# Cumulative decays in SBUF buffers of their own, and three chunks masked away from VectorE

## The chip, the cores and the metric

The kernel runs on one core of a Trainium2 chip. The metric is the device time of one execution in microseconds (us). Before the change the median of three runs is 357.06 us (356.91 to 357.37). The profile shown is one execution of 357.22 us; its instructions span 355.1 us.

## The reference

Two layers stand behind one another. The first is a gated linear attention over 4 batches, 8 heads, 768 steps and head size 48. The second is a channel mix with widths 384 and 1024.

```python
f = 1.0 / (1.0 + np.exp(-f_logit))
for t in range(S):
    state = f[:, :, t, :, None] * state + np.einsum('bhd,bhe->bhde', k[:, :, t], v[:, :, t])
    y[:, :, t] = np.einsum('bhd,bhde->bhe', q[:, :, t], state)
# x is y with its heads side by side; x_prev is x one step earlier (0 for the first)
xk = mu_k * x + (1.0 - mu_k) * x_prev
xr = mu_r * x + (1.0 - mu_r) * x_prev
k = np.maximum(xk @ w_k, 0.0)
out = sigmoid(xr @ w_r) * (k * k @ w_v)
```

All of it is float32; mu_r and w_r are drawn 8 times as large as the other inputs of their kind, so the kernel keeps each matrix operand as a high and a low part and multiplies three of the four combinations.

## The kernel before

**Chunks.** The 768 steps of a batch are cut into 6 chunks of 128, so there are 24 chunks, numbered i. A chunk's tiles have 128 partitions (two heads) by 4 pairs by 128 steps, that is 512 float32 for each partition. For a chunk the tasks are, with the names that the code gives them: `b` (L240) is a scan on VectorE that multiplies the gates up to cumulative decays; `bl` (L243, L244) copies its last column; `ln` and `rb` (L246, L248) on ScalarE make the reciprocal of the decays; `q` (L250) multiplies q by b; `kr` (L258, L259) multiplies k by the reciprocal, on GpSimd as a rule; `n` and `k` (L270, then three instructions at L262 and L266) correct that reciprocal with one Newton step, where `n` writes its product over b. Then TensorE transposes k (`TR`, L310), a copy takes it out of PSUM (`kt`, L314 or L315), and `SP` (L325, L345) makes the scores of the chunk with itself and the state's increment in `pss`. `m` (L337) masks the scores on VectorE and writes them to `ss`. For chunks below AWAY, ScalarE copies the scores out (L332), and `mg` on GpSimd masks them in SBUF (L334). `za`, `zb`, `T` (L290, L296, L302) carry the state, `YA` and `YB` (L362) make y in `py`, and `y` (L394 on ScalarE, L396 on VectorE) takes it out.

**Units.** Three chunks are a unit u of 384 steps; there are 8. Six small transfers per unit (`sp`, L452) spread y into x. The mix is `d` (L464), `xm` (L482; L477 and L474 for unit 0), the high part `xh` (L491 or L490), the low part `xl` (L497, GpSimd). TensorE makes 8 blocks `F` of nine 128x384 matrix products each, 3 blocks `R` of nine, and 6 half blocks `W` of twelve (all at L505). Between F and W the result is rectified, squared and split (`r` L528 or L529, `h` L533, `kk` L535 or L537, `l` L543 on GpSimd). `o` (L595) is the last product.

**Weights.** They arrive as 64 bit words. Eighteen pieces (8 of wk, 4 of wr, 6 of wv) are turned into float32 by three VectorE instructions, S, T and X (L623, L632, L635), then split by ScalarE (`H`, L638) and GpSimd (`L`, L642). `F`, `R` and `W` of the first unit wait for their pieces.

**PSUM.** Of eight banks, `pss` and `py` hold two each. The other four are the shared pool `pm`, from which a task takes a bank: b of a chunk from its scan to the last instruction of `k`; the transposed k; d; each word piece from S to X; each F, R and W block.

**Order.** Every engine's order is fixed when the program is made. `Plan.schedule` simulates the five queues (P TensorE, V VectorE, A ScalarE, G GpSimd, Q the SyncE queue of the DMAs). It takes, time after time, the task that can start first, in steps of 0.15 us; ties go to the lower `place`. Places are given in units: `ga = i/3 - LEAD - GATE` for the front of a chunk, `at = i/3 - LEAD` for its back, `u - PREP` for the mix, and WORDS and PLACE for weights and single loads. A task with several ways (engine, time, port flag) takes the one with the lowest end plus `DEAR` of its engine. With the port flag set, a VectorE task is lengthened by half of what GpSimd still has to run, at most to double. HAND and DRAIN are the planner's allowances for a semaphore and for TensorE's results. From chunk TIED on, `YB` waits for the next chunk's `SP`, so that small products stand together. Idle TensorE time that the planner foresees early in the program is filled with products of the identity (L700).

Of the kernel before, what the change touches and what calls it, by code (L numbers as in the profile page):

```python
# [33 lines left out]
BUFS = {  # L34
    "pm": (4, [512]), "rb": (2, [NP, C]), "ss": (2, [2, NP, C // 2]), "ktk": (2, [NP, 2, D]), "v": (3, [H, D]),
    "x": (3, [KJ, 1 + UT]), "stage": (2, [1, UT]), "xm": (4, [UT]), "r": (2, [UT]), "kk": (2, [UT]),
# [6 lines left out]

LEAD, GATE, PREP = 1.669, 0.274, 0.51
WORDS = {"wk": (-0.282, 0.023), "wr": (-4.892, 0.005), "wv": (-0.241, 0.052)}
HAND, DRAIN = 0.136, 0.465
TURN = {(True, False): 0.125, (False, True): 0.2}
TIED = 8
FILL = (14.0, 0.85)
LATE = {"sp": 3.3, "qk": 1.9}  # L50
BUNDLE = True
AWAY = 1
SPLIT = True
HALVED = 1
PLACE = {"f1": -0.627, "f2": 0.21, "sf2": -1.016, "qk0": 0.854, "qk1": -0.278, "qk2": 0.127, "qk3": 0.31, "v0": -0.151, "v1": -0.224, "cst": 0.482, "mu": 0.138, "f3": -1.807}
CHECK = (2.0, 0.2)
DEAR = {"V": 2.498, "A": 2.512}


class Plan:  # L60
# [23 lines left out]
    def schedule(self, trace=None):  # L84
        free = {"P": 0.0, "V": 2.2, "A": 0.0, "G": 1.0, "Q": 0.7}
# [22 lines left out]
        while ready:  # L108
            best = None
            for n, names in ready.items():  # L110
                _, place, ways, _, takes, _ = self.tasks[n]
                at = 0.0
                if any(not slots[b[0]] for b in takes):
                    continue
                for b in takes:
                    at = max(at, min(slots[b[0]])[0])
                at = {w[0]: max([at] + [0.0 if way_of[m] == w[0] else end[m] for m in names]) for w in ways}
                pick = min(((max(at[w[0]], free[w[0]]) + w[1] + DEAR.get(w[0], 0.0), w) for w in ways), key=lambda x: x[0])[1]
                start = max(at[pick[0]], free[pick[0]])
# [72 lines left out]
class Rwkv:  # L192


    wk = wr = wv = None
# [7 lines left out]
    def b(self, *key):  # L203
        return self.tiles[key[0]][self.slot[key]]
# [10 lines left out]
    def add_attention(self, pl, i):  # L215
# [19 lines left out]
        f = lambda: self.f_t[u % NFB][:, c]  # L235
        b = lambda: self.b("pm", ("b", i)).rearrange("p (a c) -> p a c", a=NP)
        rb = lambda: self.b("rb", i)
# [3 lines left out]
            b().rearrange(FL), f().rearrange(FL), self.low.rearrange(FL), 1.0, op0=ALU.mult, op1=ALU.max)),  # L241
            after=[f"sf{u}.{c}" if u == 0 else f"sf{u}"], takes=[("pm", ("b", i))])
        pl.add(f"bl{i}", ga, ("A", 0.2, 0, lambda: nc.scalar.copy(self.bl[:, i], b()[:, :, C - 1])),  # L243
               ("V", 0.15, 0, lambda: nc.vector.tensor_copy(self.bl[:, i], b()[:, :, C - 1])),  # L244
               uses=[("pm", ("b", i))])
        pl.add(f"ln{i}", ga, ("A", 0.63, 0, lambda: nc.scalar.activation(rb(), b(), AF.Ln)),  # L246
               after=["ex"], takes=[("rb", i)], uses=[("pm", ("b", i))])
        pl.add(f"rb{i}", ga, ("A", 0.63, 0, lambda: nc.scalar.activation(rb(), rb(), AF.Exp, scale=-1.0)),  # L248
               after=I("ln"), uses=[("rb", i)])
        pl.add(f"q{i}", ga, ("V", 0.69, 0, lambda: nc.vector.tensor_tensor(q(), q(), b(), op=ALU.mult)),  # L250
               after=I("qk"), uses=[("pm", ("b", i))])

# [8 lines left out]
        def k_b():  # L261
            nc.vector.scalar_tensor_tensor(  # L262
                k()[:, ::2], b()[:, ::2], 2.0, k()[:, ::2], op0=ALU.subtract, op1=ALU.mult)
            for h in (0, 1):
# [680 lines left out]
```

## Time and profile before

| | |
|---|---|
| median of 3 runs | 357.06 us |
| profiled execution | 357.22 us, span 355.1 us |
| busy TensorE / VectorE / ScalarE / GpSimd | 320.0 / 260.3 / 201.5 / 196.5 us |
| of TensorE: filling products | 10.8 us |
| first transpose, first F product, last o | 19.94, 51.33, 349.25 us |

The profile of one execution has a page with busy times, a strip of the span in 40 slices, the chain that ended last and the costliest groups. The trace behind it gives single instructions (start, duration, engine, line, operands, and what ended the engine's idle time in brackets), sums for chosen stretches of time, and the least, middle and largest duration of the instructions of a line. A line number is the place of the instruction in the kernel above.

### The profile page before, as it was taken

The numbers are of one execution on the slowest core, as the hardware profiler recorded it, in microseconds if no ns is written. First come the engines' busy times: TensorE is split into PE (matmuls) and PEld (weight loads), VectorE is DVE, ScalarE is ACT, GpSimd is POOL, SyncE is SP. The second block draws the span as 40 slices with busy tenths as digits, with TensorE's granted clock in tenths as the row PEclk, the third lists the DMA queues.
The fourth block names the chain that finished last, engine by engine and source line by source line (L and its number), as shares of the span: only waits on it lengthen the run. The fifth ranks groups of instructions, "written<-read, shape, count | busy, mean of one in ns | idle before, by whom it ended". The sixth has DMA issues, their size and how long they took to land.

```text
span 355.1 us, 10862 instructions
## 1 busy us (share of the span) xinstructions
PE 320.0 (90%) x4482; PEld 304.0 (86%) x4482; DVE 260.3 (73%) x526; ACT 201.5 (57%) x400; POOL 196.5 (55%) x235
## 2 busy tenths in 40 slices
PE   0294678999999999999999999999999999999993
PEld 0283567888989999999999999999999999999992
DVE  7887699989998798877999788848973943723110
ACT  3786358758367827844467537772676156605520
POOL 2555459985779357733677267725790634634400
PEclk9999899999999999999999999999999999999998
DMA  7999462336451363366323632131401100010001
GB/s 260 398 378 372 162 223 65 106 105 209 118 185 59 127 226 129 123 236 221 117 81 116 212 128 89 46 121 52 160 1 38 50 27 11 9 46 22 3 24 52
DMA packets 20650, 45.32 MB, mean 128 GB/s; under 512 B 2928, under 2 KB 13040, under 8 KB 20592
## 3 DMA queue, kind: packets, MB, share of 16 engines
q1 hardware_dynamic: 20592, 44.55, 37.0%
q8 instruction: 37, 0.61, 0.7%
q14 instruction: 21, 0.17, 0.1%
HBM read 38.64 MB, written 4.72 MB: 122 GB/s over the span
## 4 chain that ended last, share of the span: by engine, by line
PE 68%; DVE 13%; ACT 5%; issue 4%; DMA 3%; POOL 3%; SPq 1%; DVEq 0%; POOLq 0%; ACTq 0%
PE pm L505 55%; PE py L362 6%; PE pm L310 3%; PE pss L325 2%; DMA f<-in_zt 2%; DVE pm L632 2%; PE pss L345 2%; DVE pm L623 2%; POOL k2l L543 1%; DVE xm L482 1%; DVE ss L337 1%; DMA words<-in_wv 1%; DVE xm L477 1%; DVE words L635 1%; DVE xh L491 1%
## 5 line engine op out<-in xcount | busy, mean ns | idle before, releaser
L505 PE MATMUL pm<-xh,wk 128*128 128x384 f32 x384 | 105.3, 344 | 1.5 <-POOL wk L642 1.1
L505 PE MATMUL pm<-wv,k2h 128*128 128x384 f32 x384 | 98.6, 338 | 0.0
L543 POOL TENSOR_TENSOR k2l<-kk,k2h 128x384 fp32r<-128x384 f32 x64 | 68.5, 1075 | 32.2 <-DVE kk L535 16.3
L497 POOL TENSOR_TENSOR xl<-xm,xh 128x384 fp32r<-128x384 f32 x48 | 52.5, 1095 | 60.4 <-DVE xh L491 54.6
L505 PEld LDWEIGHTS pm<-xh,wk 128*128 128x128 f32 x384 | 69.8, 188 | 4.4 <-POOL wk L642 2.0
L505 PEld LDWEIGHTS pm<-wv,k2h 128*128 128x128 f32 x384 | 68.7, 188 | 0.3
L505 PE MATMUL pm<-xl,wk 128*128 128x384 f32 x192 | 64.6, 337 | 0.0
L505 PE MATMUL pm<-wv,k2l 128*128 128x384 f32 x192 | 64.5, 336 | 0.0
L528 ACT ACTIVATE r<-pm 128x384 f32<-128x384 f32 x54 | 26.5, 490 | 34.0 <-PE pm L505 33.3
L505 PE MATMUL pm<-wr,xh 128*128 128x384 f32 x144 | 38.0, 345 | 1.0 <-DVE words L635 0.9
L505 PEld LDWEIGHTS pm<-wv,k2l 128*128 128x128 f32 x192 | 36.1, 188 | 0.0
L595 DVE TENSOR_TENSOR o<-pm,lg 128x384 f32<-128x384 f32 x24 | 13.3, 553 | 31.1 <-PE pm L505 30.9
L505 PEld LDWEIGHTS pm<-xl,wk 128*128 128x128 f32 x192 | 36.1, 188 | 0.0
L535 DVE SCALAR_TENSOR_TENSOR kk<-pm,r 128x384 f32<-128x384 f32 x38 | 21.1, 554 | 20.0 <-ACT r L528 18.8
L533 ACT ACTIVATE k2h<-r 128x384 fp32r<-128x384 f32 x64 | 33.6, 524 | 3.5 <-DVE r L529 1.2
L240 DVE TENSOR_TENSOR_SCAN pm<-f,low 128x512 f32<-128x512 f32 x24 | 32.7, 1363 | 0.1
L362 PE MATMUL py<-qk,z 64*64 64x64 f32 x704 | 22.9, 230 | 10.0 <-issue 3.3
L362 PEld LDWEIGHTS py<-qk,z 64*64 64x64 f32 x704 | 16.4, 135 | 18.0 <-issue 8.8
L505 PEld LDWEIGHTS pm<-wr,xh 128*128 128x128 f32 x144 | 25.2, 188 | 1.9 <-DVE words L635 1.0
L482 DVE SCALAR_TENSOR_TENSOR xm<-pm,mu_sb,x 128x384 f32<-128x384 f32 x42 | 25.7, 612 | 0.7
L700 PE MATMUL py<-ident 128*128 128x64 f32 x72 | 10.8, 310 | 15.4 <-DMA ident<-in_cst 15.4
L505 PE MATMUL pm<-wr,xl 128*128 128x384 f32 x72 | 24.2, 336 | 0.0
(101 smaller groups left out, 559.2 us busy)
## 6 DMA issues: line engine op xcount, KB each, us to landing
qk<-in_qkt SPq DMA_DIRECT2D x24, 512.0 KB, 4.3
words<-in_wv SPq DMA_DIRECT2D x12, 512.0 KB, 3.9
f<-in_zt SPq DMA_DIRECT2D x7, 768.0 KB, 5.2
v<-in_vt SPq DMA_DIRECT2D x24, 192.0 KB, 3.1
out<-o SPq DMA_DIRECT2D x24, 192.0 KB, 2.6
words<-in_wk SPq DMA_DIRECT2D x6, 512.0 KB, 5.4
words_k2h<-in_wk SPq DMA_DIRECT2D x4, 384.0 KB, 8.6
words_k2l<-in_wk SPq DMA_DIRECT2D x4, 384.0 KB, 9.4
```

Of the source, the lines that this page charges most:

```text
L240: pl.add(f"b{i}", ga, ("V", 1.25, 1, lambda: nc.vector.tensor_tensor_scan(b().rearrange(FL), f().rearrange(FL), self.low.rearrange(FL), 1. ...
L310: nc.tensor.transpose(pk()[:, j], k()[:, j], self.ident)
L362: first[c, h] = nc.tensor.matmul(to, lhs, rhs, start=(c, h) not in first, stop=stop, skip_group_check=True)
L482: pl.add(f"xm{u}.{n}{j}", pr, ("V", 0.62, 0, lambda xm=xm, n=n, j=j: nc.vector.scalar_tensor_tensor(xm(), pm("d", u, j)[:, :UT], self.mu_s ...
L497: e.tensor_tensor(lo(), xm(), hi().bitcast(F32), op=ALU.subtract)
L505: nc.tensor.matmul(ps, lhs(a, j), rhs(bb, j), start=ends[0] and i == 0, stop=ends[1] and i == len(pr) - 1)
L528: pl.add(f"r{u}.{f}", kf, ("A", 0.5, 0, lambda r=r, ps=ps: nc.scalar.activation(r(), ps(), AF.Relu)), ("V", 0.56, 0, lambda r=r, ps=ps: nc ...
L533: pl.add(f"h{u}.{f}", kf, ("A", 0.53, 0, lambda r=r, hi=hi: nc.scalar.activation(hi(), r(), AF.Square)), after=[f"r{u}.{f}"], **kw)
L535: pl.add(f"kk{u}.{f}", kf, ("V", 0.56, 0, lambda r=r, ps=ps, kk=kk: nc.vector.scalar_tensor_tensor(kk(), ps(), 0.0, r(), op0=ALU.max, op1= ...
L543: e.tensor_tensor(lo(), kk(), hi().bitcast(F32), op=ALU.subtract)
L595: pl.add(f"o{u}.{t}", kv, ("V", 0.56, 0, lambda t=t, ps=ps, o=o: nc.vector.tensor_tensor(o(), ps(), lg()[:, t], op=ALU.mult)), after=[f"W{ ...
L700: self.nc.tensor.matmul(self.py[:, 0, 256:320], self.ident, self.ident[:, :64], start=False, stop=True, skip_group_check=True)
```

## The change

The tile b gets a pool of its own of three SBUF buffers, `"b": (3, [512])`, and no longer takes a bank of `pm`. The scan, `q`, `n` and the three instructions of `k` have the same shapes and now work on SBUF operands alone. `q` and `n` get GpSimd as a second way, with a surcharge of its own in DEAR; `q`, `n` and `k` get the port flag. AWAY rises from 1 to 3: chunks 1 and 2 are masked by ScalarE and GpSimd as chunk 0 was. The planner's numbers change with it: PREP, HAND, DRAIN, TIED, DEAR, the place of the wr pieces and the places of nine loads or gates of the start. The order of all queues is planned anew from them.

```diff
 BUFS = {
-    "pm": (4, [512]), "rb": (2, [NP, C]), "ss": (2, [2, NP, C // 2]), ...
+    "pm": (4, [512]), "b": (3, [512]), "rb": (2, [NP, C]), "ss": (2, [2, NP, C // 2]), ...
-LEAD, GATE, PREP = 1.669, 0.274, 0.51
-WORDS = {"wk": (-0.282, 0.023), "wr": (-4.892, 0.005), "wv": (-0.241, 0.052)}
-HAND, DRAIN = 0.136, 0.465
+LEAD, GATE, PREP = 1.669, 0.274, 1.542
+WORDS = {"wk": (-0.282, 0.023), "wr": (-5.255, 0.025), "wv": (-0.241, 0.052)}
+HAND, DRAIN = 0.157, 0.419
-TIED = 8
+TIED = 7
-AWAY = 1
+AWAY = 3
-PLACE = {"f1": -0.627, "f2": 0.21, "sf2": -1.016, "qk0": 0.854, "qk1": -0.278, "qk2": 0.127, "qk3": 0.31, "v0": -0.151, "v1": -0.224, "cst": 0.482, "mu": 0.138, "f3": -1.807}
+PLACE = {"f1": -0.627, "f2": -0.161, "sf2": -1.73, "qk0": 0.284, "qk1": 0.836, "qk2": -0.619, "qk3": 0.263, "v0": -0.151, "v1": -0.236, "cst": 0.345, "mu": 0.138, "f3": -2.05}
-DEAR = {"V": 2.498, "A": 2.512}
+DEAR = {"V": 3.432, "A": 2.426, "qG": 4.083, "nG": 4.943}
...
-pick = min(((max(at[w[0]], free[w[0]]) + w[1] + DEAR.get(w[0], 0.0), w) for w in ways), key=lambda x: x[0])[1]
+pick = min(((max(at[w[0]], free[w[0]]) + w[1] + DEAR.get(w[0], 0.0) + DEAR.get(n[0] + w[0], 0.0), w) for w in ways), key=lambda x: x[0])[1]
...
-        b = lambda: self.b("pm", ("b", i)).rearrange("p (a c) -> p a c", a=NP)
+        b = lambda: self.b("b", i).rearrange("p (a c) -> p a c", a=NP)
...
-            after=[f"sf{u}.{c}" if u == 0 else f"sf{u}"], takes=[("pm", ("b", i))])
+            after=[f"sf{u}.{c}" if u == 0 else f"sf{u}"], takes=[("b", i)])
...
-        pl.add(f"q{i}", ga, ("V", 0.69, 0, lambda: nc.vector.tensor_tensor(q(), q(), b(), op=ALU.mult)),
-               after=I("qk"), uses=[("pm", ("b", i))])
+        pl.add(f"q{i}", ga, ("V", 0.69, 1, lambda: nc.vector.tensor_tensor(q(), q(), b(), op=ALU.mult)),
+               ("G", 1.3, 0, lambda: nc.gpsimd.tensor_tensor(q(), q(), b(), op=ALU.mult)),
+               after=I("qk"), uses=[("b", i)])
...
-        pl.add(f"n{i}", ga, ("V", 0.69, 0, lambda: nc.vector.tensor_tensor(b(), rb(), b(), op=ALU.mult)),
-               after=I("rb") + I("q") + I("bl"), uses=[("pm", ("b", i)), ("rb", i)])
-        pl.add(f"k{i}", ga, ("V", 0.98, 0, k_b), after=I("n") + I("kr"), uses=[("pm", ("b", i))])
+        pl.add(f"n{i}", ga, ("V", 0.69, 1, lambda: nc.vector.tensor_tensor(b(), rb(), b(), op=ALU.mult)),
+               ("G", 1.3, 0, lambda: nc.gpsimd.tensor_tensor(b(), rb(), b(), op=ALU.mult)),
+               after=I("rb") + I("q") + I("bl"), uses=[("b", i), ("rb", i)])
+        pl.add(f"k{i}", ga, ("V", 0.98, 1, k_b), after=I("n") + I("kr"), uses=[("b", i)])
```

More of the change, by code (lines that the diff above doesn't have):

```diff
@@ L34 @@
 BUFS = {
-    "pm": (4, [512]), "rb": (2, [NP, C]), "ss": (2, [2, NP, C // 2]), "ktk": (2, [NP, 2, D]), "v": (3, [H, D]),
+    "pm": (4, [512]), "b": (3, [512]), "rb": (2, [NP, C]), "ss": (2, [2, NP, C // 2]), "ktk": (2, [NP, 2, D]), "v": (3, [H, D]),
     "x": (3, [KJ, 1 + UT]), "stage": (2, [1, UT]), "xm": (4, [UT]), "r": (2, [UT]), "kk": (2, [UT]),
@@ L241, in add_attention @@
             b().rearrange(FL), f().rearrange(FL), self.low.rearrange(FL), 1.0, op0=ALU.mult, op1=ALU.max)),
-            after=[f"sf{u}.{c}" if u == 0 else f"sf{u}"], takes=[("pm", ("b", i))])
+            after=[f"sf{u}.{c}" if u == 0 else f"sf{u}"], takes=[("b", i)])
         pl.add(f"bl{i}", ga, ("A", 0.2, 0, lambda: nc.scalar.copy(self.bl[:, i], b()[:, :, C - 1])),
                ("V", 0.15, 0, lambda: nc.vector.tensor_copy(self.bl[:, i], b()[:, :, C - 1])),
-               uses=[("pm", ("b", i))])
+               uses=[("b", i)])
         pl.add(f"ln{i}", ga, ("A", 0.63, 0, lambda: nc.scalar.activation(rb(), b(), AF.Ln)),
-               after=["ex"], takes=[("rb", i)], uses=[("pm", ("b", i))])
+               after=["ex"], takes=[("rb", i)], uses=[("b", i)])
         pl.add(f"rb{i}", ga, ("A", 0.63, 0, lambda: nc.scalar.activation(rb(), rb(), AF.Exp, scale=-1.0)),
                after=I("ln"), uses=[("rb", i)])
-        pl.add(f"q{i}", ga, ("V", 0.69, 0, lambda: nc.vector.tensor_tensor(q(), q(), b(), op=ALU.mult)),
-               after=I("qk"), uses=[("pm", ("b", i))])
+        pl.add(f"q{i}", ga, ("V", 0.69, 1, lambda: nc.vector.tensor_tensor(q(), q(), b(), op=ALU.mult)),
+               ("G", 1.3, 0, lambda: nc.gpsimd.tensor_tensor(q(), q(), b(), op=ALU.mult)),
+               after=I("qk"), uses=[("b", i)])
         def halves(t):
```

## The prediction

> **What bounds the kernel now.** I read the page's strip first, then sums of busy time by stretch, then the chain that ended last, then single instructions. The strip has 8.9 us in a digit.
>
> ```profile
> span 355.1 us, 10862 instructions
> ...
> PE   0294678999999999999999999999999999999993
> ```
>
> TensorE (PE) climbs for nine slices and then stays at 9. The stretches say the same in microseconds; behind the length stand the busy times of TensorE, of its weight loads, of VectorE, ScalarE and GpSimd, and at the end granted clock, DMA share and GB/s.
>
> ```profile
> 0.00:20.00 20.00, 3.71 (x17) 3.55 (x17) 16.24 (x33) 10.93 (x16) 9.04 (x18) 1.00 0.91 335
> 20.00:45.00 25.00, 16.89 (x571) 14.49 (x575) 19.32 (x45) 15.76 (x37) 11.46 (x20) 0.93 0.83 291
> 45.00:60.00 15.00, 12.25 (x204) 10.83 (x197) 14.59 (x30) 10.26 (x23) 10.88 (x12) 1.00 0.50 169
> 60.00:82.50 22.50, 20.83 (x180) 18.87 (x179) 20.84 (x37) 16.68 (x33) 20.93 (x20) 1.00 0.30 91
> 82.50:100.00 17.50, 17.32 (x268) 15.64 (x267) 16.24 (x35) 9.89 (x20) 10.40 (x14) 1.00 0.59 200
> 100.00:248.00 148.00, 147.88 (x2181) 142.81 (x2180) 123.07 (x247) 88.66 (x175) 87.79 (x103) 1.00 0.39 131
> ```
>
> From 100 us on TensorE lacks 0.12 us in 148: nothing saved on another engine there can shorten the kernel. Between 45 and 82.5 us it is idle for 37.50 - 12.25 - 20.83 = 4.42 us, and part of its busy time is the planner's filling (same columns, for the filling's line alone, TensorE first):
>
> ```profile
> 45.00:60.00 15.00, 2.90 (x24) 2.90 (x24) 1.00 0.50 169
> 60.00:82.50 22.50, 2.89 (x24) 2.96 (x24) 1.00 0.30 91
> ```
>
> So 4.42 + 5.79 = 10.2 us of that stage are no work on the result. What TensorE waits for is in the chain of waits, in order of time (start, us, what):
>
> ```profile
> 52.85 0.68 DVE words L635
> ...
> 67.61 0.56 DVE words_k2l L635
> ...
> 297.30 51.93 PE pm L505 x297
> 349.25 0.56 DVE o L595
> ```
>
> Here the chain lies on VectorE's conversion of the weights, with VectorE busy 14.59 of 15 and 20.84 of 22.5 us; near the end it is TensorE alone. **The bound is VectorE's load from 20 us to about 100 us, and TensorE after it.** A microsecond off VectorE in that stage is worth up to a microsecond, until 10.2 us are used up.
>
> **The change part by part.** *Two masks leave VectorE.* The groups of the three instructions (busy us, mean ns), and the instructions round chunk 1's mask:
>
> ```profile
> L337 DVE TENSOR_TENSOR ss<-pss,mask 128x512 f32<-128x512 f32 x23 | 15.7, 684 | 2.5 <-PE pss L345 2.2
> L334 POOL TENSOR_TENSOR ss<-ss,mask 128x512 f32<-128x512 f32 x1 | 1.3, 1272 | 4.2 <-ACT ss L332 4.2
> L332 ACT COPY ss<-pss 128x512 f32<-128x512 f32 x1 | 0.6, 585 | 0.2 <-PE pss L345 0.2
> ...
> 26.31 0.68 DVE L337 TENSOR_TENSOR ss<-pss,mask 128x512 f32<-128x512 f32 x1
> 30.50 0.63 PE L362 MATMUL py<-ss,v 64*48 64x64 f32 x32
> ```
>
> VectorE loses 2 x 0.684 = 1.37 us, ScalarE gains 1.17, GpSimd (11.46 of 25 us busy) 2.54. The masked scores of chunk 1 come 0.585 + 1.272 - 0.684 = 1.17 us later; they lie ready from 26.99 to 30.50 us, so 3.5 us cover that, and I cost it at nothing. Without the cover it would be 1.17 us for y of that chunk. What is queued behind the mask on GpSimd is `kr` of the next chunks, 1.27 us later at worst, inside the same cover.
>
> *Scan, q, n and k work in SBUF.* Three lines of before tell what this does (least, middle and largest ns), with the means of the groups:
>
> ```profile
> L464 DVE TENSOR_TENSOR pm<-x x21: 553/567/1204, 83.7 to 307.4; 128x384 f32<-128x384 f32 x21
> L240 DVE TENSOR_TENSOR_SCAN pm<-f,low x24: 1218/1226/2094, 9.3 to 258.2; 128x512 f32<-128x512 f32 x24
> L250 DVE TENSOR_TENSOR qk<-qk,pm x24: 669/677/689, 12.3 to 259.8; 128x512 f32<-128x512 f32 x24
> L692 DVE TENSOR_REDUCE least<-words x15: 536/676/687, 107.4 to 228.4; 128x1 f32<-128x512 f32 x12, 128x1 f32<-128x384 f32 x3
> ...
> L240 DVE TENSOR_TENSOR_SCAN pm<-f,low 128x512 f32<-128x512 f32 x24 | 32.7, 1363 | 0.1
> L464 DVE TENSOR_TENSOR pm<-x 128x384 f32<-128x384 f32 x21 | 14.7, 698 | 7.2 <-DMA x<-stage 6.7 <-ACT lg L562 0.3
> ```
>
> With one operand in PSUM, q never varies (669 to 689). With both inputs in SBUF, d goes up to 1204 and the scan to 2094. What they wait for:
>
> ```profile
> 113.37 1.98 POOL L543 TENSOR_TENSOR k2l<-kk,k2h 128x384 fp32r<-128x384 f32 x2
> 115.32 1.12 POOL L287 TENSOR_TENSOR g<-bl,f 128x4 f32<-128x4 f32 x1
> ...
> 114.62 1.82 DVE L240 TENSOR_TENSOR_SCAN pm<-f,low 128x512 f32<-128x512 f32 x1
> ...
> L287 POOL TENSOR_TENSOR g<-bl,f x20: 192/203/1212, 12.7 to 260.5; 128x4 f32<-128x4 f32 x20
> ```
>
> The scan issued at 114.62 ends at 116.44, 1.09 us after GpSimd's k2l has ended, and the gate of four elements that GpSimd began at 115.32 ends with the scan, where a gate takes 0.20 as a rule. The two take turns by whole instructions. The mean over the least is 1363 - 1218 = 145 ns for the scan and 698 - 553 = 145 for d. q, n and the three instructions of k join this kind. In 20 to 100 us these are, in this order for q, n and the two lines of k:
>
> ```profile
> 20.00:100.00 80.00, 4.08 (x6) 0.98 0.57 192
> 20.00:100.00 80.00, 4.81 (x7) 0.98 0.57 192
> 20.00:100.00 80.00, 3.16 (x8) 0.98 0.57 192
> 20.00:100.00 80.00, 3.82 (x16) 0.98 0.57 192
> ```
>
> 37 instructions, 37 x 0.145 = **+5.4 us** on VectorE. The low end is nothing, where GpSimd happens to rest; the high end is half of a 1.0 us GpSimd instruction at GpSimd's share there (53.67 of 80 us), 37 x 0.335 = 12.4. I take the measured mean, since the scans and d fell in the same traffic. The instructions' own length I leave as it is: reading 512 elements from SBUF alone took 676 ns (the reduction), from SBUF and PSUM 677 (q).
>
> [...]
>
> *Banks come free.* A chunk's decays no longer hold one of four banks. What this can buy is VectorE's idle time in the stage; its two large pieces are
>
> ```profile
> 36.47 0.16 DVE L382 COPY done<-py 128x2 f32<-128x2 f32 x1 [2.04 <-PE py L362]
> 44.20 0.56 DVE L315 COPY ktk<-pm 128x384 f32<-128x384 f32 x1 [1.94 <-PE pm L310]
> ```
>
> with word pieces still to be converted. Both waits are for TensorE, in an order that was fixed beforehand, so a free bank fills them only if the new order sets word work in front of them. Between 0 and -3.98 us I take the middle, **-2.0**.
>
> *More work goes to ScalarE.* DEAR was 2.498 against 2.512, a tie; now VectorE is dearer by 1.0 us, so `kt` and `xh`, which have both ways, turn to ScalarE unless it is that much later. Their VectorE time, kt in 20 to 45 us and xh in 45 to 60:
>
> ```profile
> 20.00:45.00 25.00, 1.67 (x3) 0.93 0.83 291
> 45.00:60.00 15.00, 2.94 (x5) 1.00 0.50 169
> ```
>
> Together 4.61 us; ScalarE is idle 9.2 and 4.7 us in those stretches, so it can take them. Between 0 and 4.6 I take all of kt and four of five xh: **-4.0**. GpSimd's new ways for q and n cost 1.3 + 4.083 and 1.3 + 4.943 against VectorE's 0.69 + 3.432, so they are chosen only where VectorE is 1.3 or 2.1 us behind; I count none, and both ends of that lie inside the 5.4 us above.
>
> *Places and loads.* PREP puts the mix ahead of the chunks. Unit 0's first F could start earlier, but its blocks then wait for the words of wk, which VectorE makes; under its load this is worth nothing, and shows only where VectorE falls idle. The same holds for unit 1, whose blocks stand behind W of unit 0 on TensorE. The first loads change turns on SyncE: qk1 goes back by 1.1 units; qk2, qk0, f2, f3 and the wr pieces come forward. The bytes are the same, and the queue moves 335 GB/s there (the stretch 0 to 20), so a 0.5 MB load changed about is 1.6 us early or late: 0, with 1.6 either way, mostly covered by VectorE's queue. HAND, DRAIN and TIED are only numbers of the planner.
>
> **Sum:** -1.37 + 5.4 - 2.0 - 4.0 = -2.0 us. The profiled execution took 357.22 us, which is 0.16 above the median; 357.22 - 2.0 - 0.16 = **355.1 us**.
>
> **Rivals.** *A, slower: the turns between VectorE and GpSimd become the bound.* In 45 to 82.5 us GpSimd is busy 10.88 + 20.93 = 31.8 of 37.5 us. The locked VectorE work there is 2 scans and 5 casts xh (whose least is below); one chunk's q, n and k adds, at 0.68 + 0.69 + 0.98, 2.35 us more.
>
> ```profile
> L491 DVE CAST xh<-xm x38: 351/379/1003, 46.6 to 312.2; 128x384 fp32r<-128x384 f32 x38
> ...
> 100.00:248.00 148.00, 8.23 (x12) 1.00 0.39 131
> ```
>
> 31.8 + 2 x 1.22 + 5 x 0.35 + 2.35 = 38.3 of 37.5 us: over the top by 0.8 at least. Later, 12 chunks (the row of n) bring 28 us into the 60 us that GpSimd leaves free in 148, which scan, d and xh already use. If the wait of an instruction doubles to 0.29 us, 5.4 more come on: 357.06 - 2.0 + 5.4 = **360.5 us**. The point is where the mean wait passes 0.145 + 2.0/37 = 0.20 us. For it: the planner counts half of GpSimd's rest once for k's three instructions, and no wait of GpSimd at all. Against it: part of the 37 falls in 20 to 45 us, where GpSimd is busy 11.46 of 25 us.
> [...]
>
> *B, no change: the banks were not what held it, and ScalarE's share is eaten by the turns.* Then -1.37 - 4.0 + 5.4 = 0.0: **357.1 us**. For it: the two idle pieces wait for TensorE, not for a bank.
>
> *C, much faster: the freed banks let the words be done ahead.* Most of the 10.2 us comes back, some 8: **349 us**. For it: eighteen pieces of three instructions each hold a bank; against it: they cost VectorE the same time whenever they run.
>
> [...]
>
> **How the numbers follow.** Forecast 0.45, A 0.28, B 0.14, C 0.07, D 0.06. A measurement of this kernel tells about 0.2% (0.7 us) from no change. Faster 0.45 + 0.07 + 0.06 = 0.58, same 0.14, slower 0.28. The forecast's own range is 352 to 356.3 us. The bounds of the terms reach from -1.4 - 4.0 - 4.6 = -10 (capped by the 10.2 us) to -1.4 + 12.4 = +11; 8 in 10 leaves out most of C and the far part of A: **350 to 360.5 us**.
>
> **What would show it.** Right: q, n and k spread upwards like d, by 0.1 to 0.2 us in the mean, with least values as before; VectorE's kt and xh fall in 20 to 60 us; filling plus idle of TensorE in 45 to 82.5 us falls from 10.2 to about 8; TensorE stays full after 100 us. [...]

## The result: 1.0% slower, and the profile after

The changed kernel takes 360.73 us (median of 4 runs, 359.84 to 362.36), the kernel before in the same comparison 357.22 us (4 runs, 356.91 to 358.05). The ratio is 1.010, with a 95% interval of 1.0059 to 1.0140. The forecast was 355.1 us in a range of 350 to 360.5: the sign was wrong, and the time lies at the place of rival A. The profiled execution took 359.84 us, its span is 358.0 us.

The page of the changed kernel, its busy times and its strip (a digit is 8.95 us):

```profile
span 358.0 us, 10771 instructions
...
PE 325.3 (91%) x4482; PEld 308.9 (86%) x4482; DVE 243.9 (68%) x408; ACT 246.3 (69%) x518; POOL 216.6 (61%) x237
...
PE   0397679899999999999999999999999999999993
```

VectorE is busy 16.4 us less than before (260.3), and the kernel is slower. ScalarE has 44.8 us more, GpSimd 20.1 us more. The stretches of the prediction, of the changed kernel (length; TensorE, weight loads, VectorE, ScalarE, GpSimd; granted clock, DMA share, GB/s):

```profile
20.00:45.00 25.00, 19.44 (x529) 16.88 (x528) 21.30 (x36) 15.29 (x39) 17.84 (x22) 0.90 0.74 247
45.00:60.00 15.00, 12.65 (x229) 11.90 (x228) 14.40 (x30) 11.97 (x30) 9.64 (x11) 0.82 0.61 210
60.00:82.50 22.50, 20.80 (x174) 18.34 (x173) 21.34 (x33) 18.61 (x43) 21.69 (x20) 1.00 0.30 94
100.00:248.00 148.00, 147.10 (x2161) 141.50 (x2164) 115.16 (x190) 113.99 (x240) 97.76 (x103) 1.00 0.42 135
```

Two things differ from what the prediction looked for. Between 20 and 82.5 us VectorE is as full as it was (57.04 us against 54.75 before), although masks, kt and xh have left it. And after 100 us TensorE is no longer full: it lacks 0.90 us in 148, where it lacked 0.12.

What filled VectorE is seen in the groups of the changed kernel (busy us, mean ns | idle before and who ended it) and, below, in the least, middle and largest ns of their lines:

```profile
L240 DVE TENSOR_TENSOR_SCAN b<-f,low 128x512 f32<-128x512 f32 x24 | 35.2, 1475 | 1.5 <-ACT f L573 1.5
L260 POOL TENSOR_TENSOR qk<-qk,rb 128x256 f32<-128x256 f32 x24 | 23.6, 985 | 0.0
L250 DVE TENSOR_TENSOR qk<-qk,b 128x512 f32<-128x512 f32 x24 | 23.5, 984 | 6.1 <-DMA qk<-in_qkt 5.9
L267 DVE SCALAR_TENSOR_TENSOR qk<-b,qk 128x128 f32<-128x128 f32 x48 | 23.2, 523 | 0.0
L259 POOL TENSOR_TENSOR qk<-qk,rb 128x256 f32<-128x256 f32 x24 | 22.5, 938 | 10.4 <-ACT rb L248 9.6 <-DMA qk<-in_qkt 0.6
L271 DVE TENSOR_TENSOR b<-rb,b 128x512 f32<-128x512 f32 x24 | 21.3, 887 | 4.8 <-ACT rb L248 4.1
L263 DVE SCALAR_TENSOR_TENSOR qk<-b,qk 128x256 f32<-128x256 f32 x24 | 18.3, 764 | 3.3 <-POOL qk L259 1.9
```

```profile
L250 DVE TENSOR_TENSOR qk<-qk,b x24: 665/987/1625, 13.8 to 260.3; 128x512 f32<-128x512 f32 x24
L271 DVE TENSOR_TENSOR b<-rb,b x24: 679/852/1386, 16.9 to 261.4; 128x512 f32<-128x512 f32 x24
L263 DVE SCALAR_TENSOR_TENSOR qk<-b,qk x24: 416/736/1386, 18.2 to 262.6; 128x256 f32<-128x256 f32 x24
L267 DVE SCALAR_TENSOR_TENSOR qk<-b,qk x48: 276/280/1107, 19.1 to 264.6; 128x128 f32<-128x128 f32 x48
```

The least values stand where they stood (q 669 before, 665 now), and nearly everything above them is new (the largest before were 689 for q, 697 for n, 425 and 291 for `k`): the mean of `q` is 0.32 us over its least, `n` 0.21, the first instruction of `k` 0.35, each of the other two 0.25. For a chunk that is 0.32 + 0.21 + 0.35 + 2 x 0.25 = 1.38 us, in 24 chunks 33 us of VectorE's instructions. GpSimd pays too: the halves of `kr` (L259, L260) were 0.735 and 0.748 us before and are 0.938 and 0.985.

A piece of the timeline of the changed kernel, VectorE, then GpSimd (start, us), shows who meets whom:

```profile
22.56 0.69 DVE L271 TENSOR_TENSOR b<-rb,b 128x512 f32<-128x512 f32 x1 [0.29 <-ACT rb L248]
...
24.35 0.95 DVE L263 SCALAR_TENSOR_TENSOR qk<-b,qk 128x256 f32<-128x256 f32 x1
25.22 1.54 DVE L267 SCALAR_TENSOR_TENSOR qk<-b,qk 128x128 f32<-128x128 f32 x2
```

```profile
22.61 1.23 POOL L259 TENSOR_TENSOR qk<-qk,rb 128x256 f32<-128x256 f32 x1 [3.72 <-ACT rb L248]
23.80 1.22 POOL L260 TENSOR_TENSOR qk<-qk,rb 128x256 f32<-128x256 f32 x1
24.98 0.90 POOL L259 TENSOR_TENSOR qk<-qk,rb 128x256 f32<-128x256 f32 x1
```

`n` and the first half of `kr` both wait for `rb` (the releaser in the brackets is the same, ACT rb L248), so they start 0.05 us apart: `n` goes through in its 0.69, `kr` takes 1.23 in place of 0.74. Then `k` meets the halves of the next `kr`, and its two short instructions take 1.54 us where 2 x 0.28 is their length.

Such meetings behind one event are the smaller part, though. Over the whole trace `n` and the first half of `kr` start within 0.1 us of each other in only 4 of 24 chunks, and in those `n` loses nothing (0.68 and 0.69 us). Taking every one of the five instructions that lies more than 0.05 us above its least (32.6 us in all), and the GpSimd instruction that ran when it began, 13.5 us belong to `k2l` (L545), 9.7 us to the halves of `kr`, and 9.4 us to the rest. `k2l` is work of the channel mix, released by nothing of the chunk. The last chunk's `k` meets it (GpSimd, then VectorE):

```profile
261.86 4.67 POOL L545 TENSOR_TENSOR k2l<-kk,k2h 128x384 fp32r<-128x384 f32 x4
```

```profile
263.53 2.13 DVE L267 SCALAR_TENSOR_TENSOR qk<-b,qk 128x128 f32<-128x128 f32 x2
```

Later the same waits reach TensorE (changed kernel, TensorE at 101 us; last number the idle time before and its releaser):

```profile
101.50 0.33 PE L312 MATMUL pm<-ident,qk 128*128 128x128 f32 x1 [0.40 <-DVE qk L263]
101.99 0.52 PE L312 MATMUL pm<-ident,qk 128*128 128x128 f32 x3 [0.17 <-DVE qk L267]
```

The transposes of a chunk stand still for `k`, 0.40 and 0.17 us here: the turns reach TensorE, as rival A has it.

### The profile page after: what moved, and what is told of

Its sections match the earlier page's. It is cut to its first block, busy times and chain, and to the rows that moved or that the text cites. A ratio compares the mean times of both kernels' runs of the same rounds, so it can differ in the third digit from the quotient of the medians.

```text
span 358.0 us, 10771 instructions
## 1 busy us (share of the span) xinstructions
PE 325.3 (91%) x4482; PEld 308.9 (86%) x4482; DVE 243.9 (68%) x408; ACT 246.3 (69%) x518; POOL 216.6 (61%) x237
## 4 chain that ended last, share of the span: by engine, by line
PE 69%; DVE 12%; ACT 5%; issue 4%; POOL 3%; DMA 3%; SPq 1%; DVEq 0%; POOLq 0%; ACTq 0%
PE pm L507 56%; PE py L364 6%; PE pss L327 3%; PE pm L312 2%; DMA f<-in_zt 2%; PE pss L347 2%; DVE b L240 2%; DVE qk L267 2%; DVE qk L263 2%; DVE b L271 1%; POOL wv L644 1%; POOL wk L644 1%; DMA words<-in_wv 1%; DVE xm L484 1%; DVE pm L466 1%
## 5 line engine op out<-in xcount | busy, mean ns | idle before, releaser
L545 POOL TENSOR_TENSOR k2l<-kk,k2h 128x384 fp32r<-128x384 f32 x64 | 70.7, 1112 | 34.4 <-ACT kk L539 29.2
L530 ACT ACTIVATE r<-pm 128x384 f32<-128x384 f32 x64 | 31.1, 486 | 20.0 <-PE pm L507 16.8
L240 DVE TENSOR_TENSOR_SCAN b<-f,low 128x512 f32<-128x512 f32 x24 | 35.2, 1475 | 1.5 <-ACT f L573 1.5
L539 ACT ACTIVATE kk<-r 128x384 f32<-128x384 f32 x62 | 31.7, 512 | 2.1 <-POOL k2l L545 2.1
L396 ACT ACTIVATE x<-py 64x128 f32<-64x128 f32 (+1 forms) x60 | 18.5, 309 | 17.1 <-PE py L364 16.2
L492 ACT CAST xh<-xm 128x384 fp32r<-128x384 f32 x44 | 22.2, 511 | 11.4 <-DVE xm L484 10.9
L339 DVE TENSOR_TENSOR ss<-pss,mask 128x512 f32<-128x512 f32 x21 | 14.3, 682 | 21.6 <-PE pss L347 21.6
L259 POOL TENSOR_TENSOR qk<-qk,rb 128x256 f32<-128x256 f32 x24 | 22.5, 938 | 10.4 <-ACT rb L248 9.6
L292 POOL TENSOR_TENSOR z<-sm,g 128x192 f32<-128x192 f32 x20 | 13.1, 656 | 25.9 <-DVE sm L304 25.6
L250 DVE TENSOR_TENSOR qk<-qk,b 128x512 f32<-128x512 f32 x24 | 23.5, 984 | 6.1 <-DMA qk<-in_qkt 5.9
```

Of the source, the lines that this page charges most:

```text
L240: pl.add(f"b{i}", ga, ("V", 1.25, 1, lambda: nc.vector.tensor_tensor_scan(b().rearrange(FL), f().rearrange(FL), self.low.rearrange(FL), 1. ...
L250: pl.add(f"q{i}", ga, ("V", 0.69, 1, lambda: nc.vector.tensor_tensor(q(), q(), b(), op=ALU.mult)), ("G", 1.3, 0, lambda: nc.gpsimd.tensor_ ...
L259: e.tensor_tensor(k()[:, ::2], k()[:, ::2], rb()[:, ::2], op=ALU.mult)
L396: e.activation(o, i_, AF.Copy, scale=-1.0)
L492: pl.add(f"xh{u}.{n}{j}", pr, ("A", 0.51, 0, lambda xm=xm, hi=hi: nc.scalar.copy(hi(), xm())), ("V", 0.4, 1, lambda xm=xm, hi=hi: nc.vecto ...
L530: pl.add(f"r{u}.{f}", kf, ("A", 0.5, 0, lambda r=r, ps=ps: nc.scalar.activation(r(), ps(), AF.Relu)), ("V", 0.56, 0, lambda r=r, ps=ps: nc ...
```

## The experiments

Times that the text compares come from comparisons in which the kernel before ran beside the others on the same chip; its medians there were 357.22 to 357.92 us. So effects are taken as differences of ratios to before, times 357.5 us.

**What the turns cost in the new order.** In the changed kernel q, n and k become reductions that read one SBUF operand. They take as long (medians 0.687 and 0.684 us for q and n, 0.28 for k's short ones, against 0.677, 0.686 and 0.280 in the kernel before), their products are left out, nothing else is edited, and the queues have the same order.

```diff
-("V", 0.69, 1, lambda: nc.vector.tensor_tensor(q(), q(), b(), op=ALU.mult)),
+("V", 0.69, 1, lambda: nc.vector.tensor_reduce(q()[:, :, 0], b(), axis=mybir.AxisListType.X, op=ALU.max)),
...
-            nc.vector.scalar_tensor_tensor(
-                k()[:, ::2], b()[:, ::2], 2.0, k()[:, ::2], op0=ALU.subtract, op1=ALU.mult)
...
+            for kh, bh in ((k()[:, ::2], b()[:, ::2]), *((halves(k())[:, :, h], halves(b())[:, :, 1 - h]) for h in (0, 1))):
+                nc.vector.tensor_reduce(kh[:, :, 0], bh, axis=mybir.AxisListType.X, op=ALU.max)
...
-("V", 0.69, 1, lambda: nc.vector.tensor_tensor(b(), rb(), b(), op=ALU.mult)),
+("V", 0.69, 1, lambda: nc.vector.tensor_reduce(b()[:, :, 0], rb(), axis=mybir.AxisListType.X, op=ALU.max)),
```

> The changed kernel in its own order, but q, n and the three instructions of k are reductions over one SBUF operand of the same size, with the same tiles written and waited for: they need not take turns with GpSimd. Their arithmetic is left out, so the output is not the reference's. Theory T (the turns of q, n and k with GpSimd made the change slow): 353 to 356 us, least and mean duration of these five lines within 0.03 us of each other, the first F product 2 us earlier or more. Rival O (the new order itself is slow: the gates of unit 2 stand ahead of chunk 1 on ScalarE, and ScalarE carries more): 359.5 us or more.

It took 356.87 us (356.00 to 357.80), ratio to before 0.9979 (0.9963 to 0.9996). In the profile without the turns, the least, middle and largest ns of two lines, and then the stretch after 100 us (columns as above):

```profile
L250 DVE TENSOR_REDUCE qk<-b x24: 675/687/691, 13.8 to 256.0; 128x4 f32<-128x512 f32 x24
...
L259 POOL TENSOR_TENSOR qk<-qk,rb x24: 723/734/1659, 16.6 to 255.9; 128x256 f32<-128x256 f32 x24
```

```profile
100.00:248.00 148.00, 148.00 (x2194) 142.96 (x2193) 96.92 (x191) 113.96 (x242) 85.97 (x108) 1.00 0.41 133
```

`q` doesn't wait (675 to 691 ns), the middle of `kr` is back at 0.734, VectorE has 18.2 us less in that stretch (96.92 against 115.16), and TensorE is full. Over the whole span VectorE is busy 211.1 us without the turns against 243.9. So the turns of q, n and k cost 1.0100 - 0.9979 = 1.2%, **4.3 us** (2.8 to 5.9, an estimate from the two intervals). The time lies 0.9 us above the band that the theory of turns had given, and far from its rival's 359.5. The same number says something about the other steps: without these turns the new order, its masks, its banks and its ScalarE share are only 0.2% (0.75 us) faster than before.

**Early or late chunks.** The same edit for chunks 0 to 5 only (shown for k), and with `i >= 6` for chunks 6 to 23 only.

```diff
+            if i < 6:
+                for kh, bh in ...
+                    nc.vector.tensor_reduce(kh[:, :, 0], bh, axis=mybir.AxisListType.X, op=ALU.max)
+                return
```

> As no_turns, but only for chunks 0 to 5; the arithmetic of their q, n and k is left out. Theory T, where the turns cost in the chain of the first chunks: at least two thirds of what no_turns gains. If the turns cost in the stage of the weights and later: at most a third of it. Rival O: 359.5 us or more.

> As no_turns, but only for chunks 6 to 23; the arithmetic of their q, n and k is left out. Theory T with the cost in the first chunks: at most a third of what no_turns gains, TensorE's idle time after 100 us (about 1 us) gone. With the cost later: at least two thirds. Rival O: 359.5 us or more.

Early alone: 359.31 us, ratio 1.0038 (1.0017 to 1.0060). Late alone: 357.62 us, ratio 1.0001 (0.9982 to 1.0020). The early chunks are worth 0.6%, the late ones 1.0%. The two add up to somewhat more than the whole, within their intervals. The early part is half of the whole, between the two expectations; the late part is over two thirds. The cut is not the stage's: `q` of chunks 6, 7 and 8 starts at 73.97, 84.91 and 98.27 us, so the late part has some of the stage that the prediction had called the bound.

**Which instruction.** Only k, and only n, as reductions.

```diff
-                nc.vector.scalar_tensor_tensor(kh, bh, 2.0, kh, op0=ALU.subtract, op1=ALU.mult)
+                nc.vector.tensor_reduce(kh[:, :, 0], bh, axis=mybir.AxisListType.X, op=ALU.max)
```

```diff
-nc.vector.tensor_tensor(b(), rb(), b(), op=ALU.mult)
+nc.vector.tensor_reduce(b()[:, :, 0], rb(), axis=mybir.AxisListType.X, op=ALU.max)
```

> The changed kernel in its own order; only the three instructions of k are reductions over one SBUF operand, their arithmetic left out. In the changed kernel's profile their mean lies 0.85 us per chunk over the least, of 1.37 for q, n and k together. Theory S (the turns collide because one result releases both engines: rb releases n and kr, the first half of kr releases k's first instruction while GpSimd goes on to the second half): about 60% of the 3.9 us that no_turns gained, 358 to 359 us. Rival U (all five instructions suffer alike, by chance meetings): three fifths of the instructions, so the same, but then q and n keep their mean waits; under S those of n fall too little to matter and kr keeps 1.2 us where n stands beside it.

> The changed kernel in its own order; only n is a reduction over one SBUF operand, its arithmetic left out. Theory S: the first half of kr, released by the same rb, falls back to 0.73 us from 0.94 in the mean and k is released earlier; gain 0.6 to 1.5 us (359.2 to 360.1). Rival U: one fifth of 3.9, 0.8 us, with the mean of kr unchanged.

Without the waits of `k` 357.49 us, ratio 0.9998 (0.9980 to 1.0016); without those of `n` 358.74 us, ratio 1.0025 (0.9994 to 1.0057). `k` is worth 1.0% and `n` 0.75%, together more than the 1.2% of all: whichever is taken out, the halves of `kr` that remain find less in their way (0.878 and 0.962 us without k's, 0.829 and 0.892 without n's), and the rest is shortened too. So no single instruction holds the cost. Both times are lower than either theory had given. `q` keeps its wait without k's (1.00 us in the mean), as the rival of chance meetings had said; the first half of `kr` falls without n's, but to 0.829 us and not to 0.73, as the theory of one event had said. So neither theory holds alone.

**The move alone, in the old order.** The kernel before with one edit: b lies in SBUF buffers. Every queue keeps its order. (Chunk 3's b takes the tile lg, which is unused so early.)

```diff
-        b = lambda: self.b("pm", ("b", i)).rearrange("p (a c) -> p a c", a=NP)
+        b = lambda: (self.tiles["lg"][0].rearrange(FL)[:, :512] if i == 3 else self.bs[i % 3]).rearrange("p (a c) -> p a c", a=NP)
...
+    k.bs = [cp.tile([P, 512], F32, name=f"b{i}") for i in range(3)]
```

> The kernel before with every engine's order unchanged; only the tile b lies in SBUF (three buffers in turn, chunk 3 in a buffer that is idle then). Nothing is left out. Theory T: slower than before by 2.5 to 5 us (360 to 362), with mean waits of q, n and k of 0.2 to 0.3 us each. Rival O: within 1 us of before, since the order is the old one.

372.83 us (371.96 to 374.13), ratio 1.042 (1.0389 to 1.0451): **15 us slower**, far outside both expectations. The busy times of its page, then two groups:

```profile
PE 329.8 (89%) x4482; PEld 312.1 (84%) x4482; DVE 292.4 (79%) x526; ACT 202.4 (54%) x400; POOL 214.1 (58%) x235
```

```profile
L505 PE MATMUL pm<-wr,xh 128*128 128x384 f32 x144 | 40.5, 364 | 9.4 <-DVE kk L535 7.5 <-DVE words L635 1.8
L543 POOL TENSOR_TENSOR k2l<-kk,k2h 128x384 fp32r<-128x384 f32 x64 | 71.7, 1126 | 33.6 <-DVE kk L535 21.9 <-ACT k2h L533 8.9 <-ACT kk L537 2.6
```

VectorE has 32 us more than in before (260.3), and in the old order it makes 38 of the 64 `kk`: `R` on TensorE waits 7.5 us for them, and as late as in 248 to 292 us TensorE is idle 2.49 of 44 us:

```profile
248.00:292.00 44.00, 41.51 (x571) 39.32 (x571) 35.54 (x66) 24.80 (x47) 24.97 (x27) 1.00 0.22 69
```

Then the same with q, n and k as reductions (diff as above), so that old order, SBUF buffers and free banks stay and the turns go.

> Before's order, decays in SBUF (372.83 us so), with q, n and k of every chunk as reductions of one SBUF operand, which take as long and wait for nobody: their products are left out. If the 15 us of the move are all turns: 356 to 358.5 us, the 357.6 of before or, if a bank freed earlier helps without a new order (step 3), up to 2 us less. If SBUF costs in another way too (ln and rb of ScalarE, kr of GpSimd): 361 us or more.

358.55 us (356.21 to 360.06), ratio 1.0022 (0.9994 to 1.0051). Of the 15 us, 14.2 are turns. And banks that come free earlier, at an unchanged order, gain nothing that can be told from zero; what they are worth under an order planned for them, this run can't say.

**What the new order rescues.** The move in the old order, plus the masks of chunks 1 and 2 away, plus all xh, kk, kt (but the first two), r and y of VectorE on ScalarE.

```diff
+        if way[0] == "V" and acts and (n[:2] in ("xh", "kk", "kt") and n not in ("kt0", "kt1") or n[0] in "ry"):
+            way = acts[0]
+        order += [(n, w, s) for w in (k.away[n] if n in ("m1", "m2") else [way])]
```

> Before's order with the decays in SBUF (372.83 us so), and in addition masks of chunks 1 and 2 away from VectorE, and every xh, kk, kt (but kt0, kt1), r and y that VectorE had made by ScalarE. Nothing is left out. If it is VectorE's smaller load that rescues 12 of the 15 us in the change: 360 to 364 us. If it is the order (which instructions meet GpSimd's): 369 us or more. Between: both.

368.05 us (367.65 to 368.64), ratio 1.0284 (1.0259 to 1.0310). It falls between the two expectations. The busy times of its page:

```profile
PE 325.7 (89%) x4482; PEld 309.4 (84%) x4482; DVE 246.6 (67%) x405; ACT 245.9 (67%) x521; POOL 216.8 (59%) x237
```

246.6, 245.9 and 216.8 us against 243.9, 246.3 and 216.6, and still 1.8% (6.6 us) slower. So of the 11.4 us (1.042 to 1.010) which the change takes back, moving the work gives 4.9 and the order the rest. The order doesn't do it by fewer waits. What q, n and k lie over their least values adds up to 29.8 us in the move alone, 38.1 us with the work moved too, and 32.9 us in the changed kernel: as much waiting costs 14.2 us in the old order and 4.3 in the new one, so what differs is where it falls. Which waits of the old order reach TensorE is seen for `kk` alone.

**Step 1 alone.** Before's order, decays in PSUM, only the masks of chunks 1 and 2 by ScalarE and GpSimd; and the reverse, the changed kernel with these two masks back on VectorE.

```diff
+            ("A", 0.59, 0, lambda: nc.scalar.copy(ss(), s4(self.pss[:, :, :256]))),
+            ("G", 1.35, 0, lambda: nc.gpsimd.tensor_tensor(ss(), ss(), mask(), op=ALU.mult)),
...
+        order += [(n, w, s) for w in (k.away[n] if n in ("m1", "m2") else [way])]
```

The reverse:

```diff
+    order = [(n, k.masked[n] if n in ("m1", "m2") else way, s) for n, way, s in plan.schedule() if n not in ("mg1", "mg2")]
```

> The kernel before in its own order, b in PSUM as it was; only the masks of chunks 1 and 2 are made as the change makes them, by ScalarE's copy and GpSimd. Nothing is left out. By the prediction's step the two are hidden and free VectorE by 1.37 us: 356 to 357.5 us. If GpSimd's mask holds up kr of the next chunks: 358.5 or more.

> The changed kernel in its own order; only chunks 1 and 2 are masked by VectorE again, in the place of ScalarE's copy, and GpSimd's two masks are gone. Nothing is left out. If the masks belong to the loss (1.27 us each on a GpSimd that VectorE now waits for): 359 us or less. If they are hidden: within 0.7 us of 360.7. If they help: 361.5 or more.

Alone: **355.99 us** (355.34 to 358.10), ratio 0.9974 (0.9953 to 0.9995), 0.9 us faster by the ratio, 1.6 by the medians. In the changed kernel their return makes no difference that can be told: 360.24 us, ratio 1.0092 (1.0053 to 1.0131), against 1.010.

**Step 4 alone.** Before's order, decays in PSUM, nine xh of units 0 and 1 and kt of chunks 4, 6 and 8 moved from VectorE to ScalarE; the same with the masks; and xh without kt, without and with the masks.

```diff
+        if way[0] == "V" and acts and (n[:2] == "xh" and n[2] in "01" or n in ("kt4", "kt5", "kt6", "kt7", "kt8")):
+            way = acts[0]
```

> Before's order and decays in PSUM; only xh of units 0 and 1 and kt of chunks 4 to 8 that VectorE had (9 xh, 3 kt) are made by ScalarE. Nothing is left out. Theory (step 4 of the prediction: 4.6 us less on VectorE from 20 to 80 us comes off the end): 353 to 355.5 us. Rival (ScalarE is late there or VectorE's relief is met by a wait for TensorE): 356.5 to 358 us, no change. Slower than 358 would mean that ScalarE's queue, which also makes r and kk, became the late one.

> masks_alone (355.99 us) and acts_alone together: before's order, decays in PSUM, chunks 1 and 2 masked by ScalarE and GpSimd, 9 xh and 3 kt moved to ScalarE. Nothing is left out. If the two reliefs of VectorE add: 352 to 355.3 us. If TensorE's own chain takes over after the first 1.5 us: 355.5 to 356.5 us, no better than the masks alone.

xh and kt: 359.80 us (358.39 to 360.80), ratio 1.0052 (1.0035 to 1.0069), **slower by 1.9 us**; on top of the masks 359.07 us, ratio 1.0028 (1.0005 to 1.0051), outside both expectations. Only the last sentence of the first expectation had this case. A stretch of the kernel with xh and kt moved, and what ScalarE and, in the fence after it, TensorE did next (start, us, engine):

```profile
60.00:82.50 22.50, 21.13 (x184) 19.52 (x183) 19.15 (x35) 17.09 (x34) 21.06 (x20) 1.00 0.32 95
```

```profile
82.65 1.47 ACT L571 ACTIVATE f<-f 128x1536 f32<-128x1536 f32 x1
84.13 1.28 ACT L573 ACT_TABLE_LOAD   x1
85.42 0.48 ACT L314 COPY ktk<-pm 128x384 f32<-128x384 f32 x1
```

```profile
83.42 0.69 PE L325 MATMUL pss<-qk 64*64 64x64 f32 x32
85.96 0.57 PE L345 MATMUL pss<-v,ktk 64*48 64x48 f32 x32 [1.84 <-ACT ktk L314]
```

VectorE is relieved by 20.84 - 19.15 = 1.7 us here, as meant. But the copy of chunk 6's transposed k (the next expectation calls it chunk 8's, which was a miscount) now stands behind ScalarE's sigmoids and their table loads, begins at 85.42 us, and TensorE idles 1.84 us for it. In before VectorE made that copy at 82.62.

```diff
-        if way[0] == "V" and acts and (n[:2] == "xh" and n[2] in "01" or n in ("kt4", "kt5", "kt6", "kt7", "kt8")):
+        if way[0] == "V" and acts and (n[:2] == "xh" and n[2] in "01"):
```

> Before's order, decays in PSUM; only the 9 casts xh of units 0 and 1 that VectorE had are made by ScalarE; kt stays. Nothing is left out. If the 2.9 us of step 4's xh come off the end: 354.2 to 356.3 us. If acts_alone lost its time only by kt of chunk 8 behind ScalarE's sigmoid, and the xh give nothing: 356.8 to 358 us. If xh on ScalarE (0.50 us each against 0.38) are themselves late for F: 358.3 us or more.

> masks_alone (355.99 us) and xh_alone together. Nothing is left out. If the two reliefs add: 353 to 355.2 us. If the masks' 1.6 us is all that VectorE's relief can give before TensorE's own chain: 355.5 to 356.5 us. If xh on ScalarE are late: 357 us or more.

xh alone: 357.06 us (356.02 to 357.82), ratio 0.9976 (0.9961 to 0.9990), a gain of 0.9 us by the ratio, though the median alone lies in the expectation's band for no gain. With the masks: 355.94 us (355.62 to 357.06), ratio 0.9961 (0.9939 to 0.9983). That is the best of all these kernels by its median, faster than before and after, though not to be told from the masks alone. The difference of the two shows kt's part: 1.0052 - 0.9976 is a loss of 0.76%, 2.7 us, for three copies of 0.5 us.

**The late start.** In the changed kernel the first F product begins at 55.6 us, 4.25 us later than before. There ScalarE does the sigmoid of f2 with its table loads between the two halves of chunk 1's reciprocal (17.43 to 21.5 us). One move puts it behind chunk 2's reciprocal.

```diff
+    sf2 = order.pop(names.index("sf2"))
+    names.remove("sf2")
+    order.insert(names.index("rb2") + 1, sf2)
```

> The changed kernel with one move: ScalarE's sigmoid of f2 and its two table loads (4.05 us) stand behind the reciprocal of chunk 2 instead of between the two halves of chunk 1's. Nothing is left out. If the late start (k of chunk 1 done at 26.8 us against 20.7 in the kernel before, first F product 4.25 us later) carries to the end: 357.5 to 359.7 us. If the start is made up behind TensorE's fillings: 360 to 361.5 us, as the change itself.

359.60 us (359.20 to 361.35), ratio 1.0056 (1.0033 to 1.0079). The first F product comes 1.15 us earlier (54.43). The interval overlaps that of the change, so a gain of some 0.4% is likely but not shown; the late start is not the main cost. What holds the first F product back beyond these 1.15 us is in part the turns (53.66 us without them); the rest is not shown. VectorE shows no wait for qk1 between 8 and 56 us, so a late qk1 is not part of it there.

## Why the prediction was wrong, step by step

The conclusion failed on its sum, and two errors of opposite sign are in it: the gains were forecast at 7.4 us and came to 0.75, and the turns were forecast at 5.4 us and cost 4.3 at the end. The gains decided the sign.

**Two masks (-1.37 us): right.** They give 0.9 us by the ratio where VectorE binds, and their longer way stayed covered. In the changed kernel they give nothing that can be told.

**Scan, q, n and k in SBUF (+5.4 us): the mechanism right, the wait too small, the place too narrow.** The least values stayed: q's went from 669 to 665 ns, n's from 681 to 679, those of `k` from 400 to 416 and from 272 to 276. The chances give 0.06 to D, operands that are cheaper in SBUF; no run shows such a gain. The mean wait of 0.145 us was carried over from the scan and d. Over the whole kernel it is 1.38 us for five instructions, 0.28 each. In the stage of the prediction (the groups of n, q and the two lines of k in 20 to 100 us of the changed kernel) it is about the same:

```profile
L271 DVE TENSOR_TENSOR b<-rb,b 128x512 f32<-128x512 f32 x8 | 6.9, 863 | 1.0 <-ACT rb L248 0.8
L250 DVE TENSOR_TENSOR qk<-qk,b 128x512 f32<-128x512 f32 x7 | 6.4, 916 | 0.1
L263 DVE SCALAR_TENSOR_TENSOR qk<-b,qk 128x256 f32<-128x256 f32 x7 | 6.1, 873 | 0.2
L267 DVE SCALAR_TENSOR_TENSOR qk<-b,qk 128x128 f32<-128x128 f32 x14 | 5.9, 460 | 0.0
```

Over the least values that is 8 x 0.184 + 7 x 0.251 + 7 x 0.457 + 14 x 0.184 = 9.0 us in 36 instructions, 0.25 each: past rival A's point of 0.20, and 3.6 us more than the step's 5.4. The step took the wait as a fixed price of an instruction, and it isn't one. The scan, which took turns already, waited 0.145 us in before, 1475 - 1207 = 0.27 in the changed kernel, and 1371 - 1210 = 0.16 there without the turns of q, n and k (its group without them):

```profile
L240 DVE TENSOR_TENSOR_SCAN b<-f,low 128x512 f32<-128x512 f32 x24 | 32.7, 1371 | 1.5 <-ACT f L570 1.5
```

For `d` the waits are 0.12 with these turns and 0.09 without. So the instructions that joined lengthened the waits of those already there. At the end of the kernel the turns cost 4.3 us in the new order, less than the 5.4 forecast, since of VectorE's 33 us of waits most don't reach the end, and 14.2 us in the old order, above the step's high end of 12.4. There VectorE also made `kk`, for which `R` waits; with `kk` and the rest on ScalarE 4.9 us come back, and the remaining difference is not explained by it.

**Banks come free (-2.0 us): no gain shows.** With the old order and no turns the freed banks gave +0.8 us (-0.2 to +1.8). In the new order their part isn't measured by itself: without the turns masks, ScalarE, banks and order together make -0.75. Rival B had doubted the step: the idle pieces waited for TensorE.

**More to ScalarE (-4.0 us): this is the step that failed most.** ScalarE took even more than forecast (all 64 `r`, 62 of 64 `kk`, 44 of 48 `xh`, 23 of 24 `kt`), VectorE's load fell, and no gain came of it. Alone, nine xh gave 0.9 us where four were to give 2.35, and kt lost 2.7 us. (The kt that the step had counted were those of chunks 0, 1 and 4; moved alone were 4, 6 and 8, so that kt's loss is shown for the kind, not for the same three. Nor is it a loss of the changed kernel: the one copy that VectorE keeps there is chunk 6's, made at 84.4 us, so the wait of 1.84 us doesn't arise in it.) So the runs show that the step's size was wrong and how such a move can fail. What eats the gain in the changed kernel stays open, but for the last 0.9 us that the table below shows. The step had asked whether ScalarE has idle time in the stretch (9.2 and 4.7 us). It should have asked what stands in front of the copy in ScalarE's fixed order: one group of sigmoids with its table loads (80.3 to 85.4 us) holds that queue for 5 us. At the end of the changed kernel ScalarE's copy `lg` makes TensorE idle as well (TensorE, changed kernel):

```profile
309.63 0.62 PE L507 MATMUL pm<-wv,k2h 128*128 128x384 f32 x2 [0.57 <-ACT lg L564]
```

**"A microsecond off VectorE is worth up to a microsecond, until 10.2 us are used up": too strong.** This premise carried steps 3 and 4. Filling and idle time of TensorE in 45 to 82.5 us did fall, from 10.2 to 37.50 - 12.65 - 20.80 + 4.79 = 8.84 us, close to the 8 that was named as a sign of success. The sums of the filling's line in the changed kernel (TensorE first) are

```profile
45.00:60.00 15.00, 2.79 (x24) 2.76 (x24) 0.82 0.61 210
60.00:82.50 22.50, 2.00 (x16) 2.07 (x16) 1.00 0.30 94
```

The kernel still was slower. Counting the large products (F, R and W, 1368 in each trace), their starts in us, each column from one profiled execution, show where:

| product | before | after | after, no turns | masks alone | xh and kt alone |
|---|---|---|---|---|---|
| 1st | 51.33 | 55.58 | 53.66 | 50.29 | 52.43 |
| 145th | 88.88 | 90.22 | 88.25 | 87.31 | 92.27 |
| 401st | 147.41 | 149.43 | 146.17 | 145.74 | 150.56 |
| 1001st | 278.12 | 280.27 | 276.47 | 276.43 | 281.26 |
| 1201st | 319.70 | 322.74 | 318.94 | 318.08 | 322.80 |
| last | 348.88 | 351.91 | 348.11 | 347.25 | 351.98 |

The change starts 4.25 us late, has made up 2.9 of it by the 145th product (that is what the 8.84 shows), loses 0.8 more up to the 1001st, and 0.9 from there to the 1201st. Without the turns the late start is 2.3 us and all of it is made up; the last 0.9 is lost there too (42.47 us between these two products in both, 41.58 in before). It belongs to the new order, the 0.57 us of `lg` among it, and not to ScalarE's share as such: in the old order with as much work on ScalarE the same stretch takes 41.59 us. The columns also show where the turns cost. The changed kernel lies 1.92 us behind its copy without turns at the first product, 1.97 at the 145th, 3.26 at the 401st and 3.80 from the 1001st on. So half of the cost arises after the 145th product, which starts at 90 us, and the step had counted turns up to 100 us alone; TensorE's full row after 100 us said that nothing could be saved there, not that nothing could be lost. A good sign in one stage didn't tell about the end.

**Places and loads (0, with 1.6 either way).** The sigmoid of f2 lies here: its place sf2 came forward from -1.016 to -1.73, which the step doesn't mention. Putting it later gave at most some 1.6 us (1.0100 - 1.0056), inside the bound; it isn't settled.

**Rival A came true in mechanism and sign, and its number by luck.** It forecast 360.5 us as gains of 7.4 against turns of 10.8. Measured are gains of 0.75 against turns of 4.3. Of q the traces show waits only where both inputs lie in SBUF: 665 to 1625 ns so, 675 to 691 as a reduction of one SBUF input, 669 to 689 with the other input in PSUM. A single input alone doesn't tell, however: the cast `xh` has one and went from 351 to 1003 ns in the kernel before; why, these runs don't show.

## What to carry to other kernels

Before an operand of a VectorE instruction moves from PSUM to SBUF, count everything that GpSimd has to run beside it, the other layer's work too (here 13.5 of 32.6 us of the waits began beside `k2l`). The mean wait of the instructions that took turns already (0.145 us) was too low for those that joined (0.25 to 0.28), and with them the scan's own wait rose to 0.27 us. What the waits cost was not told by their sum: 32.9 us of them cost 4.3 us in one order, 29.8 us cost 14.2 in the other. So ask of each what stands behind it in the order. A move of work to an engine with idle time needs the entries in front of it in that engine's queue, not its busy share: three copies of 0.5 us, moved to ScalarE, cost 2.7 us, and for the one that stood behind the sigmoids and their table loads TensorE idled 1.84 us. Busy time taken off VectorE was not time gained: without the turns it was busy 32.8 us less, and the kernel was 4.3 us faster. So price a relief by an instruction that ends earlier, not by the busy time saved.

## What was not expected of the hardware

The turns slowed both sides. GpSimd's halves of `kr` rose by 0.20 and 0.24 us in the mean along with VectorE's four lines, and the gate of four elements (0.20 us as a rule) took 1.12 us beside a scan of 2.02, as before. In the changed kernel, GpSimd and then VectorE:

```profile
101.69 1.01 POOL L545 TENSOR_TENSOR k2l<-kk,k2h 128x384 fp32r<-128x384 f32 x1 [0.53 <-ACT kk L539]
102.66 1.12 POOL L289 TENSOR_TENSOR g<-bl,f 128x4 f32<-128x4 f32 x1
```

```profile
101.77 2.02 DVE L240 TENSOR_TENSOR_SCAN b<-f,low 128x512 f32<-128x512 f32 x1
```

And the price of the same moved operand depended on the order far more than on the instructions: 4.3 us in one order, 14.2 us in the other, with waits of 32.9 and 29.8 us.

The granted clock in the profiles says little on the sign. In 45 to 60 us it was 1.00 before and 0.82 after, and the 128x384 products of xh and wk took 356 ns in the mean there before and 387 after, which by itself would fit a loss; but in the kernel with only the masks moved, which is faster, the row is

```profile
45.00:60.00 15.00, 14.47 (x175) 13.68 (x175) 14.52 (x28) 11.12 (x25) 12.48 (x14) 0.78 0.47 163
```

with 0.78, and without the turns it is 0.89. What sets the clock there, these runs don't show.
